# A second weight kept whole in DRAM and split on chip, and two start points moved later

## Chip, cores and metric

One Trainium2 chip, one of its cores. The metric is the device time of one execution in microseconds (us), lower is better. The kernel before takes 1595.91 us (median of 3 runs, 1595.83 to 1598.31).

## Reference

```python
def _attn_ref(q, k, v, p):            # 8 batches x 8 heads x 576 rows x 64; p has 32 rows a head
    p_packed = sm_attn(p, k, v)       # 32 rows attend to the 576 keys
    return sm_attn(q, p_packed, p_packed)

def _moe_ref(x, w_in, w_out):         # 4608 x 512, d_ff 2048
    h = x @ w_in
    return (h - np.tanh(h)) @ w_out

def _moe2_ref(x, w_in, w_out, s, b):
    r = np.maximum(x @ w_in, 0.0)
    return (s * (r * r) + b) @ w_out
```

The attention's output, with its heads laid side by side, goes through the first MLP and the result through the second. The weights arrive as 64-bit floats, which the kernel holds as pairs of 32-bit integers and converts by itself.

## The kernel before

**Numbers.** A float32 operand of a matrix product is split into a high part (rounded to the reduced format of TensorE) and the low rest, and each product is three matmuls: high by low, high by high, low by high. "Split" below means one ScalarE copy (the high part) and one VectorE subtraction (the low part).

**First half: attention and first MLP.** Eight batches run in turn, each in two halves of 288 tokens. `attention()` makes each batch's packed keys (`stage1`), its combined weights (`make_z`) and its second attention (`second_stage`). `mm1` and `mm2` are the first MLP's two products, 16 column blocks `j` for each half batch. TensorE's main stream is the loop over `j`; everything else is a Python generator of which the loop advances one step at a time through `slot()`. What order instructions get on an engine is therefore fixed when the program is built, and every engine works its list in that order.

**Weights of the first MLP.** In the first batch w_in1 and w_out1 are converted from 64 bits by `to_f32` (one ScalarE `Abs`, then four VectorE operations) while the first attention runs. `w1_steps` does w_in1, `wo1_steps` w_out1, which it also splits (`split_wo`). The first two pairs of w_out1 blocks stand in the generator `rest`, and the loop over `both([first_z(0), second_stage(0, 0)])` advances `rest` by one step for each of its own.

**Weights of the second MLP.** The second MLP uses Strassen's scheme with seven products (P1 to P7), for which seven combinations of the four blocks of each weight are needed. `second_weights()` (the generator `more`, one step in every third slot) loads 32 pieces of both weights into `w2s`, converts them into `cv`, forms the combinations, splits them and stores both parts to DRAM, in `w2_d` (w_in2, pieces 0 to 15) and `wo2_d` (w_out2, pieces 16 to 31).

**Second half: `SecondMLP`.** `run()` goes through 6 blocks of tokens by 4 steps `k`, seven products of 12 matmuls each, with w_in2's 28 units held in SBUF. Its results (`g`) go to DRAM and come back (`B<-g`) for `second()`, the product with w_out2: 6 blocks of 28 steps of 12 matmuls. During the last block of `run()` the 28 SBUF places come free one by one, and `load_unit4` fills them with units of w_out2 by DMAs that the POOL engine issues. `late(n, step)` is the part of a `run()` step that is put off into the next one: its VectorE sums, its stores of `g` and the product P4. The g buffers are reused from step to step, so a new sum waits until the store of the old one has landed.

In `second()` the inputs are split six steps ahead (`LOOK`), by `split_hi` on ScalarE and `split_lo` on VectorE.

Of the kernel before, what the change touches and what calls it, by code (L numbers as in the profile page):

```python
# [8 lines left out]
F32 = mybir.dt.float32  # L9
F32R = mybir.dt.float32r  # L10
# [3 lines left out]
ALU = mybir.AluOpType  # L14
# [4 lines left out]
def pack_attention_two_mlps(ctx, tc, q, k, v, p, w_in1, w_out1, w_in2, w_out2, s_in, b_in, out):  # L19
# [10 lines left out]
    nc = tc.nc  # L30
# [4 lines left out]
    P = 128  # L35
# [13 lines left out]
    FT = FF // (2 * P)  # L49
# [3 lines left out]
    LAND = 14  # L53
    W_K, W_P, W_PK, W_PV, W_E, W_Q = 2, 9, 5, 1, 7, 3

    AFTER, SLOTS = (3, 4, 1, 1), (0, 1, 4, 1)
    AHEAD, CATCH_UP = 13, 11
    EXP_LO, EXP_HI = 2.0 ** -15, 2.0 ** 16 * 1.875
    assert 2 * R == P and NB == 2 * C and 4 * M == P and 2 * D == P and H * D == DM

# [1 line left out]
    dram = ctx.enter_context(tc.tile_pool(name="dram", bufs=1, space=bass.MemoryType.DRAM))  # L62
# [14 lines left out]
    bias = const.tile([P, KD], F32, name="bias")  # L77
    csum = apool.tile([P, 2, P], F32, name="csum")

    w2_d = [dram.tile([7, P, 2, 2, 2, P], F32, name=f"w2_d{k}") for k in range(FT // 2)]  # L80
    wo2_d = [dram.tile([7, P, 2, 2, 2, P], F32, name=f"wo2_d{k}") for k in range(FT // 2)]
    g2_d = [[dram.tile([P, FT // 2, 2, TH], F32, name=f"g2_{i}_{n}") for n in range(7)] for i in range(NBK2)]
    x2t = dram.tile([P, KD, NT], F32, name="x2t")

# [370 lines left out]
    def both(gens):  # L455
        gens = list(gens)
        while gens:
            for g in list(gens):
                try:
                    next(g)  # L460
                except StopIteration:
                    gens.remove(g)
                    continue
                yield
# [14 lines left out]
    with tc.manual_schedule():  # L479
# [66 lines left out]
        def first_z(c):  # L546
            while ("z", c) not in granted:
                yield
            yield from make_z(0, c)
            done.add(("z", 0, c))  # L550

        def second_stage(b, hf):
            yield from scores2(b, hf)
            yield from both([stage2(b, hf, g) for g in range(G)])
            done.add(("a", b, hf))
# [49 lines left out]
        load_q(0, 1)  # L605
        until(("w1", 0, 1), conv)
        rest = seq(conv, in_turn([(wo1_steps, 0), (wo1_steps, 1)], [(wo1_steps, 2), (wo1_steps, 3)]))
        for _ in both([first_z(0), second_stage(0, 0)]):
            next(rest, None)
        nc.sync.dma_start(out=s_sb, in_=s_in.partition_broadcast(P))  # L610
        nc.sync.dma_start(out=b_sb, in_=b_in.partition_broadcast(P))

# [15 lines left out]
        def second_weights():  # L628

            both_ = wslot(I64, "w2s", [P, 8, P])
            N = 4 * FT

            def unit(n):
                if n >= 2 * FT:
                    i, f = (n - 2 * FT) // FT, n % FT
                    return w_out2, FT * P, f * P, i * P, FF // 8, f, i, wo2_d[f // 2][:, :, f % 2]
                f, i = n // 2, n % 2
                return w_in2, 2 * P, i * P, f * P, FF // 2, f, i, w2_d[f // 2][:, :, f % 2]  # L640

            def load(n):
                if n < N:
                    src, half, r0, c0, cols = unit(n)[:5]
                    for kh in range(2):
                        rr = src[kh * half + r0:kh * half + r0 + P].rearrange("p (h c) -> p h c", h=2)
                        t = both_[:, n % 2 * 4 + 2 * kh:n % 2 * 4 + 2 * kh + 2]
                        nc.sync.dma_start(out=t, in_=rr[:, :, c0:c0 + P])

            load(0)  # L650
            yield
            for n in range(N):
                out2 = n >= 2 * FT
                f, i, dst = unit(n)[5:]
                load(n + 1)
                yield
                t = both_[:, n % 2 * 4:n % 2 * 4 + 4]
                hi = t.bitcast(F32).rearrange("p a c -> p (a c)")[:, :7 * P]
                xa = cv[:, 7:11] if n % 2 else cv[:, 0:4]
                yield from to_f32(xa, t, xa.bitcast(I32))  # L660
                if out2:
                    if f == 0:
                        nc.gpsimd.memset(csum, 0.0)
                    for kh in range(2):
                        nc.gpsimd.tensor_tensor(out=csum, in0=csum, in1=xa[:, 2 * kh:2 * kh + 2], op=ALU.add)

                nc.vector.tensor_tensor(out=cv[:, 4], in0=xa[:, 1], in1=xa[:, 3], op=ALU.add)
                yield
                nc.vector.tensor_tensor(out=cv[:, 5], in0=cv[:, 4], in1=xa[:, 0], op=ALU.subtract)
                yield  # L670
                nc.vector.tensor_tensor(out=cv[:, 6], in0=xa[:, 2], in1=cv[:, 5], op=ALU.subtract)
                yield
                nc.vector.tensor_tensor(out=xa[:, 1], in0=xa[:, 0], in1=xa[:, 1], op=ALU.subtract)
                yield
                x = (cv[:, 4:11] if n % 2 else cv[:, 0:7]).rearrange("p a c -> p (a c)")
                nc.scalar.copy(hi.bitcast(F32R), x)
                yield
                nc.vector.tensor_tensor(out=x.bitcast(F32R), in0=x, in1=hi, op=ALU.subtract)
                yield
                for hl, v in enumerate((hi, x)):  # L680
                    v = v.rearrange("p (c x) -> p c x", c=7)
                    for c0, c1, at in ((0, 4, 3), (4, 7, 0)) if n % 2 else ((0, 7, 0),):
                        nc.sync.dma_start(out=dst[c0:c1, :, hl, i].rearrange("c p x -> p c x"),
                                          in_=v[:, at:at + c1 - c0])
                if out2 and f == FT - 1:
                    ps = bank_h(f"cs_{i}")
                    for h in range(2):
                        nc.tensor.matmul(ps[:, 2 * h:2 * h + 2], csum[:, h], ones, start=True, stop=True)
                    for h in range(2):
                        m = 2 * h + i  # L690
                        nc.vector.tensor_scalar(out=bias[:, m:m + 1], in0=ps[:, 2 * h:2 * h + 1], scalar1=b_sb,
                                                scalar2=None, op0=ALU.mult)
                    yield
# [59 lines left out]
        for b in range(B):  # L753
# [4 lines left out]
            for hf, js in parts:  # L758
# [10 lines left out]
                for j in js:  # L769
                    c = j // CH  # L770
# [11 lines left out]
                    t = act1(h, f"{b}_{hf}_{j}")  # L782
# [27 lines left out]
class SecondMLP:  # L810
# [21 lines left out]
    def __init__(self, tc, ctx, wslot, w2_d, wo2_d, x2t, g2_d, s_sb, bias, out):  # L832
        self.tc, self.nc, self.ctx, self.wslot = tc, tc.nc, ctx, wslot
        self.w2_d, self.wo2_d, self.x2t, self.g2_d = w2_d, wo2_d, x2t, g2_d
        self.s_sb, self.bias, self.out = s_sb, bias, out
        self.P, self.TH = 128, g2_d[0][0].shape[3]
        self.NBK, self.NK = len(g2_d), len(w2_d)

        self.units = []
        for k in range(self.NK):  # L840
            for p in self.ORDER[:2] + (("P4",) if k else ()) + self.ORDER[2:6]:
                self.units.append((k - 1 if p == "P4" else k, p))
        self.units.append((self.NK - 1, "P4"))
        self.place, self.w2, self.w4 = [], {}, {}
        self.next4 = 0
        pool = ctx.enter_context(tc.tile_pool(name="early", bufs=1, side="right"))
        self.raw = {n: pool.tile([128, 2, self.TH], F32, tag=n, name=n) for n in ("B11", "B12", "B22", "B21")}
        self.xs = [pool.tile([128, 2, 2, self.TH], F32R, tag=f"x{n}", name=f"x{n}") for n in range(4)]
        px = ctx.enter_context(tc.tile_pool(name="px", bufs=1, space=bass.MemoryType.PSUM, side="right"))
        self.X = px.tile([128, 2, 512], F32, tag="x", name="X")  # L850
# [21 lines left out]
    def load_unit4(self):  # L872

        n = self.next4
        p, k = self.ORDER4[n // self.NK], n % self.NK
        self.w4[p, k] = self.place[n]
        self.nc.gpsimd.dma_start(out=self.place[n].bitcast(F32), in_=self.wo2_d[k][self.W[p]])
        self.next4 += 1

    def slots_for(self, t):  # L880
        n = len(self.place)
# [91 lines left out]
    def run(self):  # L973
# [15 lines left out]
        for n in range(NP):  # L989
# [12 lines left out]

            def freed():
                if last:
                    self.load_unit4()

            if n:
# [94 lines left out]
    def second(self, NP):  # L1102
# [52 lines left out]
                                         start=first and p in ("P1", "P5", "P6"), stop=last, skip_group_check=True)  # L1155

        for n, (i, p, k) in enumerate(self.steps[:-self.NK]):
            while self.split < min(len(self.steps), n + self.LOOK):
                self.split_step()
            if k == 1 and outs:  # L1160
                emit(*outs.pop())
            if k == 0 and n:
                after(*self.steps[n - 1][:2])
            multiply(n, range(2))
            if n < 3:
                self.late(NP - 1, n)
            if n == 4:
                self.late(NP - 1, 3)
                self.stream += self.g[3:]
            if n >= 2 and n % 3 and self.next4 < len(self.units):  # L1170
                self.load_unit4()

        after(*self.steps[-self.NK - 1][:2])
# [40 lines left out]
```

## Time and profile before

| | |
|---|---|
| median of the runs | 1595.91 us |
| the profiled execution | 1598.22 us, of which its trace spans 1596.5 us |
| TensorE busy | 1483.3 us, 93% of the span |
| VectorE busy | 1088.6 us, 68% |
| ScalarE busy | 743.0 us, 47% |
| mean granted TensorE clock | 0.976 of full speed |

Three stretches matter. From 0 to about 210 us the first batch starts up; in the 40 us slices of the page TensorE is busy 40 to 70% there. From 210 to 1160 us it is busy nearly without a gap. From 1160 to 1250 us `run()` hands over to `second()`, and one slice there falls to 70%. After that TensorE is full again until the last stores.

### The profile page before, as it was taken

What the parts mean: (1) busy time and instruction counts of PE and PEld (TensorE: products, weight loads), DVE (VectorE), ACT (ScalarE), POOL (GpSimd) and SP (SyncE); (2) the same over time, 40 slices, a digit from 0 to 9 for tenths busy, and PEclk for the clock granted to TensorE, in tenths of its full rate; (3) what the DMA queues carried; (4) which work ended last, traced back from release to release, by engine and by line L of the source; (5) the groups of instructions that cost most, each with busy time, mean ns of one, the idle gap of its engine ahead of it and who ended that gap; (6) DMA issues with size and microseconds to landing.
All of it is one profiled execution on the core that took longest, in us unless ns stands there. A gap on an engine that the chain in (4) does not pass through costs nothing.

```text
span 1596.5 us, 27039 instructions
## 1 busy us (share of the span) xinstructions
PE 1483.3 (93%) x9976; PEld 1389.4 (87%) x9976; DVE 1088.6 (68%) x2076; ACT 743.0 (47%) x1417; POOL 108.4 (7%) x143
## 2 busy tenths in 40 slices
PE   4477799999999999999999999999997999999998
PEld 2366588898888888988899999999997999999998
DVE  4888486877879687786844677677754665565564
ACT  2444244444444444444433556566554554454452
POOL 0234100000000000000202000000021000000000
PEclk9689899999999999999999999999999899999999
DMA  8844645374554645453624664655589886786683
GB/s 163 192 133 110 128 118 145 95 165 120 117 146 120 148 111 124 142 127 109 185 98 187 237 246 181 234 218 203 220 340 394 281 235 187 219 251 187 211 252 80
DMA packets 396372, 285.70 MB, mean 179 GB/s; under 512 B 243664, under 2 KB 341968, under 8 KB 396240
## 3 DMA queue, kind: packets, MB, share of 16 engines
q1 hardware_dynamic: 387648, 254.03, 54.2%
q0 software_dynamic: 8064, 29.36, 5.0%
q8 instruction: 78, 1.28, 0.3%
q10 hardware_dynamic: 528, 0.59, 0.1%
q14 instruction: 54, 0.44, 0.1%
HBM read 168.43 MB, written 115.47 MB: 178 GB/s over the span
## 4 chain that ended last, share of the span: by engine, by line
PE 72%; DVE 10%; DMA 8%; SPq 4%; issue 3%; ACT 2%; DVEq 0%; ACTq 0%
PE acc L427 19%; PE Y L1154 9%; PE h L404 9%; PE Y L939 8%; PE Z L1154 6%; PE X L1154 6%; PE X L939 5%; PE Z L939 5%; DMA g<-g 3%; PE zp L318 2%; SPq L197 1%; DMA q<-in_q_dram 1%; DVE gl L133 1%; DMA w1s<-in_moe_w_in_dram 1%; PE pv L292 1%
## 5 line engine op out<-in xcount | busy, mean ns | idle before, releaser
L427 PE MATMUL acc<-gh,wo 128*128 128x288 f32 x2040 | 422.3, 298 | 0.0
L427 PEld LDWEIGHTS acc<-gh,wo 128*128 128x128 f32 x2040 | 333.5, 191 | 0.0
L427 PE MATMUL acc<-gl,wo 128*128 128x288 f32 x1020 | 314.7, 309 | 6.9 <-POOL gl L133 6.5
L412 ACT ACTIVATE t<-h 128x288 f32<-128x288 f32 x256 | 105.1, 410 | 306.8 <-PE h L404 264.3
L427 PEld LDWEIGHTS acc<-gl,wo 128*128 128x128 f32 x1020 | 194.5, 191 | 46.6 <-issue 31.2
L413 DVE TENSOR_TENSOR t<-h,t 128x288 f32<-128x288 f32 x256 | 115.8, 452 | 165.9 <-ACT t L412 164.9
L404 PE MATMUL h<-a2h,z 128*128 128x288 f32 x1024 | 216.4, 299 | 6.7 <-DVE z L385 6.7
L854 DVE TENSOR_TENSOR x<-B,x 128x768 fp32r<-128x768 f32 x158 | 147.1, 950 | 88.0 <-ACT x L1088 75.0
L404 PE MATMUL h<-a2l,z 128*128 128x288 f32 x512 | 155.1, 303 | 20.2 <-DVE a2l L369 18.6
L404 PEld LDWEIGHTS h<-a2h,z 128*128 128x128 f32 x1024 | 167.3, 192 | 7.3 <-DVE z L385 7.3
L939 PE MATMUL Y<-x,w 128*128 128x384 f32 x864 | 160.7, 339 | 9.0 <-DVE g L854 8.2
L939 PEld LDWEIGHTS Y<-x,w 128*128 128x128 f32 x864 | 152.7, 190 | 10.0 <-DVE g L854 8.5
L1154 PE MATMUL Y<-x,w 128*128 128x384 f32 x864 | 153.2, 335 | 0.7 <-DVE s L854 0.7
L1154 PEld LDWEIGHTS Y<-x,w 128*128 128x128 f32 x864 | 150.3, 188 | 1.0 <-DVE s L854 1.0
L404 PEld LDWEIGHTS h<-a2l,z 128*128 128x128 f32 x512 | 98.6, 193 | 26.0 <-DVE a2l L369 20.1
L1088 ACT CAST x<-B 128x768 fp32r<-128x768 f32 x116 | 93.7, 833 | 50.3 <-DMA B<-g 27.6
L939 PE MATMUL Z<-x,w 128*128 128x384 f32 x576 | 109.6, 339 | 4.4 <-DVE u L854 4.4
L132 ACT CAST gh<-t 128x288 fp32r<-128x288 f32 x255 | 108.5, 426 | 1.2 <-DVE t L413 1.2
L939 PE MATMUL X<-x,w 128*128 128x384 f32 x576 | 108.0, 336 | 0.0
L939 PEld LDWEIGHTS Z<-x,w 128*128 128x128 f32 x576 | 102.3, 191 | 4.7 <-DVE u L854 4.7
L1154 PE MATMUL X<-x,w 128*128 128x384 f32 x576 | 102.8, 337 | 0.0
L1154 PE MATMUL Z<-x,w 128*128 128x384 f32 x576 | 102.0, 335 | 0.0
(148 smaller groups left out, 2047.8 us busy)
## 6 DMA issues: line engine op xcount, KB each, us to landing
g<-g SPq DMA_DIRECT2D x196, 384.0 KB, 3.5
B<-g SPq DMA_DIRECT2D x116, 384.0 KB, 4.6
w<-w_d POOLq DMA_DIRECT2D x28, 512.0 KB, 7.2
w<-wo_d POOLq DMA_DIRECT2D x28, 512.0 KB, 8.4
k<-in_k_dram SPq DMA_DIRECT2D x128, 72.0 KB, 3.0
q<-in_q_dram SPq DMA_DIRECT2D x256, 36.0 KB, 2.1
B<-x2t SPq DMA_DIRECT2D x24, 384.0 KB, 5.4
g<-s SPq DMA_DIRECT2D x24, 384.0 KB, 2.7
```

Of the source, the lines that this page charges most:

```text
L132: nc.scalar.copy(hi, x)
L133: (eng or nc.vector).tensor_tensor(out=lo, in0=x, in1=hi.bitcast(F32), op=ALU.subtract)
L197: nc.sync.dma_start(out=t[p0:p0 + 32], in_=src.rearrange("(n r) d -> r n d", r=32))
L318: nc.tensor.matmul(ps[e][i * M:(i + 1) * M, :rhs(i).shape[-1]], pblk[b][r, h // 4, h % 4 * M:h % 4 * M + M], rhs(i)[r], start=True, stop=True)
L404: nc.tensor.matmul(h[:, :HB], zt[:, zi, g, f0:f0 + P], a[:, g], start=(n == 0), stop=(n == 3 * G - 1))
L412: nc.scalar.activation(t, h[:, :HB], AF.Tanh)
L413: nc.vector.tensor_tensor(out=t, in0=h[:, :HB], in1=t, op=ALU.subtract)
L427: nc.tensor.matmul(acc[m][:, :HB], w[:, m * P:(m + 1) * P], x, start=(j == js[0] and i == 0), stop=(j == js[-1] and i == 2))
L854: self.nc.vector.tensor_tensor(out=o, in0=a, in1=b, op=op)
L939: self.nc.tensor.matmul(bank[:, f, :self.TH], w[:, f, a, kt], x[:, b, kt], start=(p in ("P1", "P5", "P6") and m == 0), stop=(m == 5), skip ...
L1088: self.nc.scalar.copy(self.xs[(7 * self.NBK + n) % self.XS][:, 0], self.ready[0])
L1154: nc.tensor.matmul(bank[:, ft, :T], w[:, kk, u, ft], x[:, v, kk], start=first and p in ("P1", "P5", "P6"), stop=last, skip_group_check=True)
```

## The change

Three edits. First, w_out2's combinations are no longer split before they are stored: `wo2_d` holds one float32 number in place of two parts, a unit's load is 256 KB in place of 512 KB, and lands in the half of the unit's place that will be the low part. A new function `split_unit4` makes the high part of one unit on ScalarE and subtracts it on VectorE one call later. It is called before each of the later twelve `load_unit4` of `run()`, and then in `second()`. The loads in `second()` are issued in each step rather than in two of three.

Second, the loop over `first_z(0)` and `second_stage(0, 0)` begins to advance `rest` only after its first 16 steps (`FIRST`). Third, `second_weights()` waits `LAND` = 14 of its steps after its first load, in place of one.

```diff
-    AHEAD, CATCH_UP = 13, 11
+    AHEAD, CATCH_UP, FIRST = 13, 11, 16
...
-    wo2_d = [dram.tile([7, P, 2, 2, 2, P], F32, name=f"wo2_d{k}") for k in range(FT // 2)]
+    wo2_d = [dram.tile([7, P, 2, 2, P], F32, name=f"wo2_d{k}") for k in range(FT // 2)]
...
-        for _ in both([first_z(0), second_stage(0, 0)]):
-            next(rest, None)
+        for i, _ in enumerate(both([first_z(0), second_stage(0, 0)])):
+            if i >= FIRST:
+                next(rest, None)
...
             load(0)
-            yield
+            yield from wait(LAND)
...
-                nc.scalar.copy(hi.bitcast(F32R), x)
-                yield
-                nc.vector.tensor_tensor(out=x.bitcast(F32R), in0=x, in1=hi, op=ALU.subtract)
-                yield
-                for hl, v in enumerate((hi, x)):
+                if not out2:
+                    nc.scalar.copy(hi.bitcast(F32R), x)
+                    yield
+                    nc.vector.tensor_tensor(out=x.bitcast(F32R), in0=x, in1=hi, op=ALU.subtract)
+                    yield
+                for hl, v in enumerate((x,) if out2 else (hi, x)):
...
-        self.nc.gpsimd.dma_start(out=self.place[n].bitcast(F32), in_=self.wo2_d[k][self.W[p]])
+        self.nc.gpsimd.dma_start(out=self.place[n][:, :, 1].bitcast(F32), in_=self.wo2_d[k][self.W[p]])
         self.next4 += 1
+
+    def split_unit4(self):
+
+        n = self.split4
+        if n:
+            t = self.place[n - 1]
+            self.sub(t[:, :, 1], t[:, :, 1].bitcast(F32), t[:, :, 0].bitcast(F32))
+        if n < len(self.units):
+            t = self.place[n]
+            self.nc.scalar.copy(t[:, :, 0], t[:, :, 1].bitcast(F32))
+        self.split4 += 1
...
             def freed():
                 if last:
+                    if self.next4 > 2:
+                        self.split_unit4()
                     self.load_unit4()
...
         for n, (i, p, k) in enumerate(self.steps[:-self.NK]):
+            while self.split4 <= min(len(self.units), n + 4):
+                self.split_unit4()
...
-            if n >= 2 and n % 3 and self.next4 < len(self.units):
+            if n >= 2 and self.next4 < len(self.units):
                 self.load_unit4()
```

On ScalarE, at the first batch's start (`z` is the first combined weight, `wo1s` a 64-bit block of w_out1, `t_0_0_0` the softmax of the second attention), the list before reads:

```order
L96 COPY pblk_348<-pkT_0_344 128x128
L117 ACTIVATE t_395<-wo1s_201 128x512
L117 ACTIVATE t_399<-wo1s_203 128x512
L383 CAST z_0_384<-zp_0_0_385 128x512
L383 CAST z_0_384<-zp_0_1_386 128x512
L117 ACTIVATE t_417<-wo1s_205 128x512
L117 ACTIVATE t_419<-wo1s_207 128x512
L136 CAST wo_0_423<-wo1s_201 128x512
L136 CAST wo_1_425<-wo1s_203 128x512
L347 ACTIVATE t_0_0_0_439<-t_0_0_0_439 128x288
```

In the changed kernel the same place of ScalarE's list reads:

```order
L97 COPY pblk_348<-pkT_0_344 128x128
L384 CAST z_0_384<-zp_0_0_385 128x512
L384 CAST z_0_384<-zp_0_1_386 128x512
L118 ACTIVATE t_424<-wo1s_201 128x512
L118 ACTIVATE t_427<-wo1s_203 128x512
L348 ACTIVATE t_0_0_0_417<-t_0_0_0_417 128x288
L348 ACTIVATE t_0_0_1_420<-t_0_0_1_420 128x288
L118 ACTIVATE t_442<-wo1s_205 128x512
```

The casts of `z` have moved ahead of the first two reads of w_out1, and the softmax ahead of the second two.

Still on ScalarE, where the first batch ends and the second one's attention begins (`cv<-w2s` is the first step of `second_weights()`, `e_1_0` the packed attention of batch 1), the list before reads:

```order
L412 ACTIVATE t_0_15_1398<-h_0_15_1379 128x288
L132 CAST gh_0_0_15_1401<-t_0_14_1314 128x288
L117 ACTIVATE cv<-w2s 128x512
L265 ACTIVATE e_1_0_1393,nm_0_1427<-s_1_0_0_1428,nm_0_1427 128x5x32
L265 ACTIVATE e_1_0_1393,nm_0_1427<-s_1_0_0_1428,nm_0_1427 128x4x32
```

In the changed kernel the attention follows directly, and the read of `w2s` stands here, after the attention of both head groups:

```order
L368 CAST a2h_0_1782<-a_1_0_1_1776 128x288
L384 CAST z_2_1811<-zp_2_0_1812 128x512
L384 CAST z_2_1811<-zp_2_1_1813 128x512
L413 ACTIVATE t_1_14_1826<-h_1_14_1778 128x288
L133 CAST gh_0_1_14_1829<-t_1_13_1749 128x288
L118 ACTIVATE cv<-w2s 128x512
```

It has moved behind everything that the second batch's attention needs of ScalarE for its first half.

The third place is the last block of `run()` on ScalarE in the changed kernel (`g` and `u` are its squares, `s` the copy of a product, `w_0`, `w_1` pairs of units):

```order
L868 ACTIVATE g_10518<-g_10518 128x768
L891 CAST w_0_9967<-w_0_9967 128x2x256 x2
L867 ACTIVATE g_10515<-X 128x768
L868 ACTIVATE g_10515<-g_10515 128x768
L891 CAST w_1_9970<-w_1_9970 128x2x256
L867 ACTIVATE u_10514<-u_10514 128x768
L868 ACTIVATE u_10514<-u_10514 128x768
L891 CAST w_1_9970<-w_1_9970 128x2x256
```

Before, the squares followed each other there without a cast of `w` between them.

## Rows read from the trace of the kernel before

**Rows 1.** Windows: busy us of each engine, clock, DMA share, GB/s.

```profile
1200.00:1240.00 40.00, 27.85 (x149) 26.90 (x147) 19.44 (x23) 16.82 (x21) 5.28 (x10) 0.90 0.97 376
1280.00:1320.00 40.00, 40.00 (x232) 40.00 (x231) 24.49 (x30) 21.22 (x28) 0.00 (x0) 1.00 0.83 251
```

**Rows 2.** Timeline of PE, 1150 to 1250 us: start, length, instructions, [idle before].

```profile
1179.65 4.36 PE L939 MATMUL Y<-x,w 128*128 128x384 f32 x24
...
1194.29 4.36 PE L939 MATMUL Y<-x,w 128*128 128x384 f32 x24
...
1215.49 4.34 PE L939 MATMUL Y<-x,w 128*128 128x384 f32 x24
...
1240.52 4.21 PE L939 MATMUL Y<-x,w 128*128 128x384 f32 x12 [8.18 <-DVE g L854]
```

**Rows 3.** The chain that ended last, 1150 to 1260 us: start, length.

```profile
1199.44 10.28 DMA g<-g
...
1229.48 9.24 DMA B<-g
```

**Rows 4.** DMA, 1163 to 1245 us: queues as in part 3; issues, us to landing.

```profile
q1 hardware_dynamic: 5589, 15.30, 47.2%
q0 software_dynamic: 3888, 14.16, 46.7%
...
w<-wo_d POOLq DMA_DIRECT2D x27, 512.0 KB, 8.4
g<-g SPq DMA_DIRECT2D x27, 384.0 KB, 7.3
```

**Rows 5.** DMA issues, 900 to 1160 us.

```profile
g<-g SPq DMA_DIRECT2D x108, 384.0 KB, 2.6
```

**Rows 6.** The page's DMA issues, whole span.

```profile
B<-g SPq DMA_DIRECT2D x116, 384.0 KB, 4.6
...
k<-in_k_dram SPq DMA_DIRECT2D x128, 72.0 KB, 3.0
```

**Rows 7.** Timeline of POOL, last block of run().

```profile
1188.47 0.53 POOL L877 DMA_DIRECT2D w<-wo_d  x1 [1.55 <-PE Z L939]
```

**Rows 8.** DMA queues, 640 to 680 us: packets, MB, share of 16 engines.

```profile
q1 hardware_dynamic: 9675, 5.64, 49.0%
```

**Rows 9.** The page's costliest groups: VectorE's splits of inputs.

```profile
L854 DVE TENSOR_TENSOR x<-B,x 128x768 fp32r<-128x768 f32 x158 | 147.1, 950 | 88.0 <-ACT x L1088 75.0
```

**Rows 10.** Timeline of ACT, 18 to 66 us.

```profile
37.27 0.66 ACT L117 ACTIVATE t<-wo1s 128x512 f32<-128x512 f32 x1 [5.29 <-DMA wo1s<-in_moe_w_out_dram]
...
41.34 1.06 ACT L383 CAST z<-zp 128x512 fp32r<-128x512 f32 x2
...
59.33 2.19 ACT L117 ACTIVATE w<-w1s 128x1024 f32<-128x1024 f32 x2
```

**Rows 11.** Timeline of PE, 18 to 62 us.

```profile
32.13 1.52 PE L318 MATMUL zp<-w,pblk 64*32 64x512 f32 x16
...
59.61 0.61 PE L404 MATMUL h<-a2l,z 128*128 128x288 f32 x1 [11.45 <-DVE a2l L369]
```

**Rows 12.** Timeline of SP's queue, 18 to 80 us.

```profile
36.08 9.34 SPq L146 DMA_DIRECT2D w1s<-in_moe_w_in_dram  x8
```

**Rows 13.** Tile w1s, 30 to 64 us.

```profile
DMA to landing us min/median/max: 8.7/11.6/13.4
```

**Rows 14.** Timeline of ACT, 135 to 215 us.

```profile
166.98 0.66 ACT L117 ACTIVATE cv<-w2s 128x512 f32<-128x512 f32 x1 [7.92 <-DMA w2s<-in_moe_w_in_dram]
```

**Rows 15.** Timeline of PE, 155 to 180 us.

```profile
169.14 1.11 PE L272 MATMUL e1Tp<-ident,e 128*128 128x128 f32 x4 [7.38 <-ACT e L265]
```

**Rows 16.** Timeline of DVE, 135 to 215 us.

```profile
160.91 0.22 DVE L260 TENSOR_SCALAR nm<-nm 128x1 f32<-128x1 f32 x1
...
177.31 0.47 DVE L246 STREAM_TRANSPOSE kT<-k 128x288 f32<-128x288 f32 x1
```

**Rows 17.** Timeline of SP's queue, 0 to 210 us.

```profile
164.65 5.70 SPq L170 DMA_DIRECT2D k<-in_k_dram  x8
```

More of the change, by code (lines that the diff above doesn't have):

```diff
@@ L675, in second_weights @@
                 x = (cv[:, 4:11] if n % 2 else cv[:, 0:7]).rearrange("p a c -> p (a c)")
-                nc.scalar.copy(hi.bitcast(F32R), x)
-                yield
-                nc.vector.tensor_tensor(out=x.bitcast(F32R), in0=x, in1=hi, op=ALU.subtract)
-                yield
-                for hl, v in enumerate((hi, x)):
+                if not out2:
[4 more added lines that the diff above has]
+                for hl, v in enumerate((x,) if out2 else (hi, x)):
                     v = v.rearrange("p (c x) -> p c x", c=7)
                     for c0, c1, at in ((0, 4, 3), (4, 7, 0)) if n % 2 else ((0, 7, 0),):
-                        nc.sync.dma_start(out=dst[c0:c1, :, hl, i].rearrange("c p x -> p c x"),
-                                          in_=v[:, at:at + c1 - c0])
+                        to = dst[c0:c1, :, i] if out2 else dst[c0:c1, :, hl, i]
+                        nc.sync.dma_start(out=to.rearrange("c p x -> p c x"), in_=v[:, at:at + c1 - c0])
                 if out2 and f == FT - 1:
@@ L844, in __init__ @@
         self.place, self.w2, self.w4 = [], {}, {}
-        self.next4 = 0
+        self.next4 = self.split4 = 0
         pool = ctx.enter_context(tc.tile_pool(name="early", bufs=1, side="right"))
```

## Prediction

> **What bounds the kernel now.** I read the page's slices first, since they show where TensorE is not full, then the windows of those stretches, the chain that ended last inside them, and the timelines of the engine that waits and the one it waits for. TensorE runs the sum of its matmuls almost without a gap from 210 to 1160 us and from 1250 us to the end, so whatever the change adds or takes on other engines there is worth nothing unless it makes TensorE wait. Three places are left, and each edit touches one.
>
> Place one is the hand-over from `run()` to `second()`. In its 40 us TensorE is busy for 27.85 us and the DMA engines for 97% of the time at 376 GB/s [rows 1]. The chain there is not compute: it is the landing of stores of `g` (10.28 us for one) and of a load `B<-g` (9.24 us) [rows 3]. The same store takes 2.6 us while `run()` is in its steady state [rows 5] and 7.3 us here [rows 4]. What has come on top is POOL's queue: 27 loads of w_out2, 46.7% of sixteen engines' time over 82 us [rows 4]. TensorE's own rows give the loss. A pair of Y products comes every 14.64 us (1179.65 to 1194.29); the next was due at 1208.93 and came at 1215.49, 6.56 us late. Then it stands idle for 8.18 us, and the 12 matmuls after that take 4.21 us where 24 took 4.36 us, 2.0 us more than their share [rows 2]. Together 16.7 us.
>
> Place two is the start. ScalarE waits 5.29 us for a block of w_out1 and reaches the casts of `z` at 41.34 us [rows 10], although TensorE had their input done at 32.13 + 1.52 = 33.65 us; TensorE's first `h` then starts at 59.61 us after 11.45 us of idleness [rows 11]. Place three is the second batch's attention: ScalarE waits 7.92 us for the first load of w_in2 [rows 14], while the softmax behind it had its input at 161.13 us [rows 16], and TensorE stands for 7.38 us until that softmax is through [rows 15].
>
> **Term one, half as many bytes in place one.** A unit's load cost 46.7% of 16 engines over 82 us, 612.7 engine-us for 3888 packets: 157.6 ns for a packet of 3642 bytes, and 612.7/27/16 = 1.42 us of all sixteen engines a load [rows 4]. After the change a unit lands in two runs of 1 KB in each of 128 partitions, 256 pieces. No load of POOL in this trace has such pieces, so I bound their price. From below: the mixed small packets of 640 to 680 us, 5.64 MB in 9675 or 583 bytes on average, took 0.49 x 16 x 40 us / 9675 = 32.4 ns [rows 8]. From above: a whole old packet, 157.6 ns. A straight line between the two gives 50 ns at 1 KB, and since a kilobyte lies nearer to 583 bytes than to 3642 I take that. A load is then 256 x 50/16 = 0.80 us, 0.62 us less, 16.7 us less over 27 loads: of the 82 us the DMA engines had about 77 us of work (47.2% and 46.7% [rows 4]), and would have 60. With a quarter of the time free, a store should land nearer to 2.6 us than to 7.3 us, and the 6.56 us go. The 8.18 us go only in part: `second()` begins with loads `B<-g` on which ScalarE, and behind it VectorE and TensorE, must wait in order. With the page's median of 4.6 us [rows 6] in place of 9.24 us, 8.18 - 4.64 = 3.5 us of idleness stay. Term one is 16.7 - 3.5 = 13 us; its ends are 16.7 us and, if pieces cost as much as old packets, a loss (below).
>
> Here a rule can be weighed against the rows. The Trainium skill, "DMA: Bandwidth & Descriptors", sections "Anatomy of one DMA — SWDGE (gpsimd) path" and "Bandwidth", fits a POOL-issued transfer as 2.0 us fixed plus its bytes at 436 GB/s, and tells authors to batch towards 1 MiB; by that estimate 512 KB costs 3.2 us and 256 KB 2.6 us, so that halving a load saves a fifth; 27 loads would then give back 7.7 us of 82, term one would be 6 us, and the kernel would take 1580 us. The row has 1.42 us of all engines for 512 KB, less than the fit's fixed part alone, so a good part of that lies outside the engines' busy time here; none of this trace's rows shows 256 KB on POOL's queue.
>
> **What the split adds.** 28 ScalarE copies and 28 VectorE subtractions of 512 elements. VectorE takes 950 ns for 768 elements [rows 9], so 0.63 us here, 17.7 us in all, and ScalarE's copies I put no higher. Sixteen steps of `second_weights()` lose a copy and a subtraction of 896 elements each in return, under a full TensorE, worth nothing. The cover of the added work: 17 splits fall into 17 steps of `second()`, 17 x 2.09 = 35 us of TensorE (14.64/7 us for a product), where VectorE was busy 24.49 of 40 us [rows 1]; 21.7 + 10.7 = 32 of 35 us still fits, and inputs are split six steps ahead. Eleven or twelve fall into the last block of `run()`, whose idle VectorE time was itself waiting for stores. A copy waits for its load on an engine that works in order, and behind it stand the squares that `late` and P4 need. But it is called three `freed()` later than its load, and 15 such calls in four passes of 14.64 us are 3.9 us apart: 11.7 us against 8.4 us to landing when the queues were full [rows 4]. I cost this at nothing, up to 2 us. Where `load_unit4` stands in `second()` doesn't matter: POOL has nothing else to do, and issues when TensorE gives up a place [rows 7].
>
> **Term two, FIRST.** ScalarE meets the casts of `z` before it waits for w_out1. At most the chain to the first `h` moves up by 41.34 - 33.65 = 7.7 us. VectorE still has all four conversions to do, and TensorE needs w_out1 soon after, but that work fills waits. The next limit is a transfer that compute doesn't move: the second quarter of w_in1, issued from 36.08 to 45.4 us [rows 12] and landing 11.6 us later [rows 13], is there at 57.0 us; its conversion began its second half at 59.33 + 2.19/2 = 60.4 us [rows 10]. So 3.4 us at least for the second combined weight if everything else keeps pace. I take 4 us, ends 0 (VectorE, which was nearly full, gives it back) and 7.7.
>
> **Term three, LAND.** ScalarE's wait leaves the path: the read of `w2s` goes behind the second batch's attention, and lands long before it is due. The gain is at most TensorE's 7.38 us. What is late next is the second head group's `k`: its eight DMAs were issued from 164.65 us for 5.70 us [rows 17], 0.71 us each; without the second piece's two DMAs ahead of them they end at 168.9 us, land 3.0 us later [rows 6], and two transposes (0.94 us) end at 172.9 us where they ended at 177.78 us [rows 16]: 4.9 us. Between 4.9 and 7.4 I take 6. The conversion moved behind that point meets a full TensorE and costs nothing.
>
> **Sum.** 13 + 4 + 6 = 23 us. The profiled execution took 1598.22 us, 1596.5 us of it span; its span becomes 1573.5 us and its own time 1575. The median of the runs is 2.3 us below that execution, so I forecast 1595.9 - 23 = 1573 us.
>
> **Rivals.** *The queues stay full.* A piece of 89 ns would make a load cost what it did (1.42 x 16/256). At 70 ns, halfway from my 50, a load takes 1.12 us, 27 loads give back 8 us rather than 16.7, the DMA engines still have 69 of 82 us of work, and stores still land late. Term one shrinks to 13 x 8/16.7 = 6 us: 1580 us. For it speaks that no such load is in the trace; against it that small packets cost little at 640 us [rows 8]. The page of the Trainium skill named above would come out at the same time.
>
> *The start gives its gains back.* VectorE's list in the first 160 us has the same work in another order. If terms two and three come to nothing, 1583 us; with term three at 4.9 us alone, 1578 us. Against it: all three waits are on transfers, not on a full engine.
>
> *Pieces cost as much as packets (slower).* 256 x 157.6/16 = 2.52 us a load, 1.10 us more, 30 us over 27 loads in a stretch without room: minus the 10 us of the start, 20 us slower, 1616 us. It decides from 0.37 us more a load, 112 ns a piece, which is over three times the small packets of rows 8.
>
> *It doesn't matter.* Everything is hidden elsewhere, 1594 to 1598 us. TensorE's waits in all three places name what the edits remove, so this is unlikely.
>
> **Chances and range.** My forecast with its own spread of 1565 to 1577 us: 0.60. Queues full (1577 to 1583): 0.15. Start given back (1577 to 1585): 0.12. More than forecast (below 1565): 0.05. No change: 0.04. Slower: 0.04. The range 1564 to 1584 us leaves out about 0.15. A measurement of this kernel can tell 0.2%, 3.2 us, from no change; by the cases faster 0.92, same 0.04, slower 0.04.
>
> **What would show it.** Right: 28 loads of 256 KB on POOL's queue with a share well under 30% of the same stretch, stores `g<-g` back to 3 to 4 us, no idleness over 4 us on TensorE between 1160 and 1240 us; first `h` on TensorE at 52 to 56 us; no wait of ScalarE for `w2s`, and e1Tp less than 2 us after the matmuls before it. Wrong: ScalarE waiting in `split_unit4` for `wo_d`, VectorE's subtractions of `w` ahead of a TensorE wait, a share of POOL's queue as before, or TensorE idle at 70 to 100 us for w_out1 that is now converted too late.

## The result, and the profile after

The changed kernel takes 1571.16 us (median of 4 runs, 1569.75 to 1572.55) beside 1595.87 us for the kernel before (4 runs, 1593.48 to 1598.31): a ratio of 0.9845, 95% interval 0.9826 to 0.9864, or 24.7 us less. The profiled execution took 1572.55 us, 1570.8 us of it span.

First the hand-over. Windows of the changed kernel, with the columns of [rows 1]:

```profile
1160.00:1200.00 40.00, 40.00 (x232) 40.00 (x231) 28.08 (x34) 25.14 (x34) 13.75 (x20) 1.00 0.96 351
1200.00:1240.00 40.00, 35.87 (x197) 35.55 (x197) 27.48 (x34) 25.73 (x37) 2.97 (x5) 0.96 0.88 312
1240.00:1280.00 40.00, 40.00 (x232) 40.00 (x232) 33.32 (x47) 25.38 (x39) 0.00 (x0) 1.00 0.76 218
```

TensorE is full up to 1200 us, and the worst 40 us hold 35.87 us of work in place of 27.85 [rows 1]. VectorE, which now splits w_out2 too, is busiest behind that, 33.32 of 40 us, while TensorE has no gap there. TensorE's timeline of the same stretch:

```profile
1165.47 4.36 PE L953 MATMUL Y<-x,w 128*128 128x384 f32 x24
...
1194.75 4.36 PE L953 MATMUL Y<-x,w 128*128 128x384 f32 x24
...
1203.11 2.27 PE L953 MATMUL Y<-x,w 128*128 128x384 f32 x12
1205.22 6.40 PE L1170 MATMUL X<-x,w 128*128 128x384 f32 x36
1215.75 3.92 PE L953 MATMUL Y<-x,w 128*128 128x384 f32 x12 [4.13 <-DVE g L857]
```

The pairs of Y keep their 14.64 us (two of them from 1165.47 to 1194.75), so the 6.56 us of lateness [rows 2] are gone. The stall before the last P4 is 4.13 us in place of 8.18, and those 12 matmuls still run slow, 3.92 us where half of 4.36 would be 2.18. The window of those 12 matmuls (PEclk, the granted clock, is the third number from the end) has it at 0.56, most of the stretch at the lower of the two levels (1.2 and 2.4 GHz), right behind 4.13 us without work:

```profile
1215.75:1219.60 3.85, 3.85 (x13) 3.85 (x14) 2.21 (x3) 3.12 (x4) 0.00 (x0) 0.56 0.35 140
```

The chain that ended last shows what the stall is:

```profile
1204.95 8.03 DMA B<-g
...
1214.75 0.96 DVE g L857
1215.75 3.92 PE Y L953 x12
```

No store of g stands there any more [rows 3]; one load B<-g does, at 8.03 us. The DMA view, 1138 to 1230 us, with the columns of [rows 4]:

```profile
q1 hardware_dynamic: 7664, 20.94, 59.5%
q0 software_dynamic: 2240, 7.34, 25.7%
...
g<-g SPq DMA_DIRECT2D x34, 384.0 KB, 4.7
w<-wo_d POOLq DMA_DIRECT2D x28, 256.0 KB, 5.8
B<-g SPq DMA_DIRECT2D x14, 384.0 KB, 6.3
```

These are 92 us, and [rows 4] are 82 us. The line of POOL's queue in the kernel before over 92 us, 1154 to 1246 us, is:

```profile
q0 software_dynamic: 3888, 14.16, 41.6%
```

So over equal lengths POOL's queue takes 25.7% in place of 41.6%. A store of g takes 4.7 us in place of 7.0 (7.3 in [rows 4]).

At the start, ScalarE's timeline has the cast of z ahead of the waits for w_out1 [rows 10], and TensorE's first h comes 7.5 us earlier than in [rows 11]:

```profile
34.91 1.07 ACT L384 CAST z<-zp 128x512 fp32r<-128x512 f32 x2 [2.63 <-PE zp L319]
37.40 0.70 ACT L118 ACTIVATE t<-wo1s 128x512 f32<-128x512 f32 x1 [1.41 <-DMA wo1s<-in_moe_w_out_dram]
```

```profile
52.10 0.61 PE L405 MATMUL h<-a2l,z 128*128 128x288 f32 x1 [13.88 <-DVE a2l L370]
```

In the second batch ScalarE reads w2s 30 us later and without a wait, and TensorE's idleness of 7.38 us [rows 15] is 1.06 us. Timelines of ScalarE, TensorE and VectorE, in that order:

```profile
196.50 0.70 ACT L118 ACTIVATE cv<-w2s 128x512 f32<-128x512 f32 x1
```

```profile
157.65 0.66 PE L273 MATMUL e1Tp<-ident,e 128*128 128x128 f32 x4 [1.06 <-ACT e L266]
...
167.09 1.57 PE L229 MATMUL s<-kT,ppT 128*64 128x288 f32 x6 [2.01 <-DVE kT L247]
```

```profile
163.79 0.84 DVE L247 STREAM_TRANSPOSE kT<-k 128x288 f32<-128x288 f32 x2 [1.60 <-DMA k<-in_k_dram]
...
166.56 0.48 DVE L247 STREAM_TRANSPOSE kT<-k 128x288 f32<-128x288 f32 x1 [1.93 <-DMA k<-in_k_dram]
```

What is late next is the second head group's k, as the forecast said.

### The profile page after: what moved, and what is told of

It reads as the page before. It is cut to its first block, busy times and chain, and to the rows that moved or that the text cites. A ratio compares the mean times of both kernels' runs of the same rounds, so it can differ in the third digit from the quotient of the medians.

```text
span 1570.8 us, 26999 instructions
## 1 busy us (share of the span) xinstructions
PE 1483.8 (94%) x9976; PEld 1391.6 (89%) x9976; DVE 1091.3 (69%) x2088; ACT 742.1 (47%) x1429; POOL 115.2 (7%) x143
## 4 chain that ended last, share of the span: by engine, by line
PE 76%; DVE 11%; SPq 4%; DMA 4%; issue 3%; ACT 2%; POOL 0%; ACTq 0%; DVEq 0%
PE acc L428 18%; PE Y L1170 10%; PE Y L953 9%; PE h L405 9%; PE Z L1170 6%; PE X L953 6%; PE Z L953 6%; PE X L1170 6%; PE zp L319 2%; SPq L198 2%; DVE gl L134 1%; PE pv L293 1%; SPq L171 1%; PE s L229 1%; DVE t L414 1%
## 5 line engine op out<-in xcount | busy, mean ns | idle before, releaser
L134 DVE TENSOR_TENSOR gl<-t,gh 128x288 fp32r<-128x288 f32 x224 | 103.8, 464 | 0.0
```

The costliest lines, as they stand in the source:

```text
L134: (eng or nc.vector).tensor_tensor(out=lo, in0=x, in1=hi.bitcast(F32), op=ALU.subtract)
```

## The experiments

The theory is the forecast's: three separate waits, each worth its own term. The rivals are that the terms overlap, that the hand-over gained by something other than bytes, and that the added split costs something. Each kernel ran beside the kernel before on the same chip (four or five runs each; the kernel before has seven to nine):

| kernel | median us | before us | ratio, 95% interval |
|---|---|---|---|
| float32 w_out2 alone | 1583.43 | 1596.57 | 0.9920, 0.9907 to 0.9934 |
| start edits alone | 1586.42 | 1596.57 | 0.9938, 0.9926 to 0.9951 |
| changed, FIRST undone | 1576.16 | 1596.57 | 0.9878, 0.9864 to 0.9892 |
| changed, LAND undone | 1580.40 | 1596.57 | 0.9905, 0.9891 to 0.9919 |
| units loaded twice | 1582.26 | 1596.34 | 0.9918, 0.9904 to 0.9931 |
| inputs loaded earlier | 1574.27 | 1596.34 | 0.9860, 0.9846 to 0.9873 |
| that, and k ahead of q | 1568.18 | 1596.34 | 0.9821, 0.9807 to 0.9834 |
| split done twice | 1581.11 | 1596.34 | 0.9904, 0.9890 to 0.9917 |
| sum ahead of the splits | 1567.44 | 1595.42 | 0.9826, 0.9811 to 0.9841 |
| that, and k ahead of q | 1563.46 | 1595.42 | 0.9801, 0.9785 to 0.9817 |
| no split | 1573.25 | 1595.42 | 0.9866, 0.9849 to 0.9883 |
| loads in two of three steps | 1571.59 | 1596.63 | 0.9848, 0.9830 to 0.9867 |

### The parts by themselves

Only the edits to w_out2, with both start points as before:

```diff
-    AHEAD, CATCH_UP, FIRST = 13, 11, 16
+    AHEAD, CATCH_UP, FIRST = 13, 11, 0
...
-            yield from wait(LAND)
+            yield
```

> Only the float32 copy of w_out2 and its split; both start points as before. If the 11 us that the changed kernel's trace shows between 1165 us and the end belong to the lighter loads: 1585 us, stores of g in the hand-over at 4 to 5 us, the first 500 us as before. If the 3.7 us gained between 210 and 835 us come from the pieces of w_out2 that lost two steps (they begin at about 500 us): 1581 us. Rival, the gain in the hand-over came from the earlier start (other phase of the transfers): 1594 to 1598 us.

Measured: 13.1 us less, 1583.43 us, between the 1585 and the 1581 us of the first two cases. The opposite kernel keeps the old w_out2 and has the two start points alone:

> Only FIRST = 16 and LAND = 14; w_out2 stored split as before. If the start's gains reach the end: 1585.4 us (10.5 us less), with the idle times in the hand-over as before (some 8 us before a half-speed Y, stores of g at 7 us). If the 3.7 us of the steady state come from the new order at the start too: 1582 us. Rival, the start gives its gains back: 1590 to 1596 us.

Measured: 10.2 us less, as in the first case. 13.1 and 10.2 make 23.3 us, the whole change gives 24.7 us, and the intervals (some 2 us each) cover the difference: the start's gain reaches the end, and the parts add. The hand-over behaves accordingly. TensorE's timeline of the kernel with w_out2 alone, then of the one with the start alone:

```profile
1224.95 3.58 PE L953 MATMUL Y<-x,w 128*128 128x384 f32 x12 [4.22 <-DVE g L857]
```

```profile
1227.97 3.79 PE L940 MATMUL Y<-x,w 128*128 128x384 f32 x12 [8.02 <-DVE g L855]
```

Without the lighter loads the 8 us stall is there, whatever the start did.

A smaller part of the 13.1 us lies elsewhere. One window, 600 to 835 us, of the kernel before, of the start alone, of w_out2 alone and of the changed kernel; the pieces of w_out2 are made in this stretch:

```profile
600.00:835.00 235.00, 230.09 (x1804) 209.25 (x1803) 170.13 (x441) 101.82 (x268) 22.27 (x33) 1.00 0.47 128
```

```profile
600.00:835.00 235.00, 230.08 (x1806) 209.83 (x1805) 175.12 (x440) 103.71 (x269) 22.83 (x35) 1.00 0.48 135
```

```profile
600.00:835.00 235.00, 231.64 (x1816) 212.40 (x1815) 158.35 (x419) 93.51 (x258) 20.51 (x31) 0.99 0.40 107
```

```profile
600.00:835.00 235.00, 232.09 (x1839) 213.54 (x1838) 163.63 (x424) 95.54 (x263) 23.16 (x35) 1.00 0.41 113
```

With unsplit pieces alone VectorE has some 12 us and ScalarE 8 us less to do, and TensorE is busy for 1.6 to 2.0 us more in the same 235 us. That is small, but it is in both kernels with the lighter pieces and in neither of the others. A window at fixed times holds slightly different work in each kernel, so a cut by events is safer.

Such a cut is the store of `x2t`, the tile in DRAM in which the first half leaves its output. SP's queue issues 17 of them in each kernel, and the first and the last split each profiled execution into three parts, of which the third holds `run()` and `second()`. The last of them, before and then changed:

```profile
832.59 0.57 SPq L445 DMA_DIRECT2D x2t<-xs  x1
```

```profile
818.41 0.53 SPq L446 DMA_DIRECT2D x2t<-xs  x1
```

| kernel | us to the first store | first to last | last to the end of the span |
|---|---|---|---|
| before | 108.08 | 724.51 | 763.9 |
| start edits alone | 103.03 | 718.16 | 762.0 |
| float32 w_out2 alone | 105.31 | 722.21 | 752.5 |
| changed, FIRST undone | 105.56 | 715.87 | 752.6 |
| changed, LAND undone | 102.35 | 722.48 | 752.2 |
| changed | 102.54 | 715.87 | 752.4 |

The last column separates the kernels with the lighter loads from the others: 9.6 to 11.4 us. The middle one gives the lighter pieces 2.3 us in both pairs (724.51 - 722.21 and 718.16 - 715.87).

Then the changed kernel with one start point undone at a time, by the two lines of the diff above.

> The changed kernel with FIRST = 0. If the cast of z behind the wait for w_out1 is worth what the changed trace shows (about 5.3 us at 140 us): 1576.5 us, first h at 59 to 60 us again. Rival, the two start edits overlap, and the later one would have made up for the first: 1571 to 1573 us.

> The changed kernel with the wait of LAND steps undone. If the wait of ScalarE for w_in2's first load was on the path for its whole size less what comes behind it (about 5.2 us): 1576.4 us, ScalarE waiting some 8 us for w2s ahead of the softmax. Rival, the steady state has room to make it up: 1571 to 1573 us.

Measured: FIRST undone costs 5.0 us (1576.16 beside 1571.16), first h at 58.37 us; LAND undone costs 9.2 us, more than the 5.2 us expected. These two differences set runs beside each other that were not made together. Set against w_out2 alone, on the same chip, FIRST is worth 1583.43 - 1580.40 = 3.0 us and LAND 1583.43 - 1576.16 = 7.3 us. The spans of the profiled executions (w_out2 alone 1580.0, LAND undone 1577.0, FIRST undone 1574.0, changed 1570.8) give 3.0 and 3.2 us for FIRST, 6.0 and 6.2 us for LAND. The table agrees with the smaller figures: up to the first store FIRST gives 3.0 us in both pairs (105.31 - 102.35 and 105.56 - 102.54) and nothing more behind it, and LAND gives 6.3 to 6.6 us between the first and the last store. So FIRST is worth about 3 us and LAND 6 to 7 us (3 to 5 and 6 to 9 by the medians), and neither makes up for the other.

FIRST moves the first h by 58.37 - 52.10 = 6.3 us, twice what it is worth. The products `zp` of the second combined weight, for which TensorE waits until VectorE has converted w_in1's second quarter, move by 2.4 us only. TensorE's timeline with FIRST undone, then changed:

```profile
67.69 1.09 PE L319 MATMUL zp<-w,pblk 64*32 64x512 f32 x16 [1.39 <-DVE w L128]
```

```profile
65.26 1.09 PE L319 MATMUL zp<-w,pblk 64*32 64x512 f32 x16 [0.69 <-DVE w L128]
```

With LAND undone ScalarE's wait and TensorE's behind it are back (timelines of ScalarE and TensorE):

```profile
160.89 0.66 ACT L118 ACTIVATE cv<-w2s 128x512 f32<-128x512 f32 x1 [7.19 <-DMA w2s<-in_moe_w_in_dram]
```

```profile
163.05 1.11 PE L273 MATMUL e1Tp<-ident,e 128*128 128x128 f32 x4 [6.65 <-ACT e L266]
```

### Bytes, or something else?

Each unit is loaded a second time into the half that the high part then overwrites:

```diff
+        self.nc.gpsimd.dma_start(out=self.place[n][:, :, 0].bitcast(F32), in_=self.wo2_d[k][self.W[p]])
         self.nc.gpsimd.dma_start(out=self.place[n][:, :, 1].bitcast(F32), in_=self.wo2_d[k][self.W[p]])
```

> The changed kernel, but each unit of w_out2 is loaded twice, once into the half that the high part then overwrites: 512 KB a unit again, in 256 KB loads, and nothing else changed. If the bytes of these loads in the hand-over are what the float32 copy saves: POOL's queue at or over its old 47% in the hand-over, stores of g at 7 us or more, and the 11 to 13 us come back: 1582 to 1586 us. Rival, the gain comes from the order of the loads or the pieces of the store: 1570 to 1573 us.

Measured: 1582.26 us, 11.1 us more than the changed kernel. The DMA view of 1138 to 1230 us, and TensorE's timeline:

```profile
q0 software_dynamic: 4320, 14.16, 41.4%
...
w<-wo_d POOLq DMA_DIRECT2D x56, 256.0 KB, 7.9
g<-g SPq DMA_DIRECT2D x30, 384.0 KB, 6.7
```

```profile
1195.81 3.81 PE L954 MATMUL Z<-x,w 128*128 128x384 f32 x12 [5.09 <-DVE u L857]
...
1224.57 4.21 PE L954 MATMUL Y<-x,w 128*128 128x384 f32 x12 [8.15 <-DVE g L857]
```

14.16 MB are on POOL's queue again, as in [rows 4], and both old stalls are back, although the pieces, the split and the order of the loads are the changed kernel's. Its share of 41.4% is that of the kernel before over an equal 92 us, 41.6%; the 47% expected was taken from 82 us. From the last store of `x2t` to the end the kernel takes 764.1 us, as the kernel before does (763.9). ScalarE never waits for a unit of w_out2 there, so the second load doesn't act by holding up the split. The traffic of these loads is what the hand-over gained by. The number of loads isn't it, since 28 loads before and 56 here give the same stalls; bytes and packets go up together (3888 packets before, 2240 changed, 4320 here), and the runs don't tell these two apart.

### Does the added split cost anything?

First each ScalarE copy and each VectorE operation of the split is doubled, without changing the numbers; then both are left out (the bodies of `split_unit4` do nothing, and the second product is taken with parts of w_out2 that are not the right ones).

```diff
             self.sub(t[:, :, 1], t[:, :, 1].bitcast(F32), t[:, :, 0].bitcast(F32))
+            self.add(t[:, :, 1], t[:, :, 1].bitcast(F32), t[:, :, 1].bitcast(F32), ALU.max)
...
             self.nc.scalar.copy(t[:, :, 0], t[:, :, 1].bitcast(F32))
+            self.nc.scalar.copy(t[:, :, 0], t[:, :, 1].bitcast(F32))
```

> The changed kernel with the added split done twice: 28 more copies on ScalarE and 28 more operations of the same size on VectorE (0.6 us each), same result. If the split is hidden under TensorE, as the forecast costed it: 1569 to 1573 us. Rival, VectorE has no room there: up to 18 us more, 1575 to 1589 us.

> The changed kernel without the added split: the high and low parts of w_out2 are left as whatever lies there, so the second product is left wrong in its values while its matmuls stay. If the split is hidden, as the forecast costed it: 1569 to 1573 us. Rival, part of it lies on the path in the hand-over, where doubling it cost 9.5 us: 1562 to 1568 us.

Measured: doubled 1581.11 us, 10 us more; left out 1573.25 us, no gain, and just above the 1569 to 1573 us of the first case. From the last store of `x2t` to the end the kernel without a split takes 752.3 us, as the changed one does (752.4), and the doubled one 763.6 us. One split of each unit is hidden, two aren't. The window and TensorE's timeline of the doubled kernel show where the cover ends:

```profile
1240.00:1280.00 40.00, 35.80 (x183) 33.86 (x182) 35.59 (x50) 28.43 (x46) 0.00 (x0) 0.91 0.62 178
```

```profile
1271.94 8.98 PE L1172 MATMUL Y<-x,w 128*128 128x384 f32 x34 [2.79 <-DVE w L857]
```

VectorE at 35.59 of 40 us makes TensorE wait for the subtraction of w itself. The expectation's first theory, that double would be hidden too, failed: the cover was there once and was nearly used up by that.

The loads of `second()` in two of three steps again (`n % 3` put back into the condition):

> The changed kernel with the loads in second() issued in two of three steps again. If POOL's loads start only when TensorE gives up a place, and TensorE needs a unit many steps later, as the forecast argued: 1569 to 1573 us. Rival, the later loads hold up ScalarE's copies of the split, and behind them the inputs: 1575 us or more, with ScalarE waiting for wo_d.

Measured: 1571.59 us, the same. Whether these loads are issued in each step or in two of three makes no difference here.

### What remains of the stall

If B<-g comes late, it should help to load it earlier: `free_loads` is set for the whole last step of `run()`.

```diff
+            self.free_loads = last and end
...
-        self.free_loads = True
```

> The changed kernel, but the inputs of second() from the fifth on are loaded during the last step of run() as buffers come free, not only from the start of second(). If the 4.1 us of idleness and the half-speed Y behind it (1.8 us) come from the late load B<-g: 4 to 6 us less, 1565 to 1567 us. Rival, the earlier loads only delay the stores of g, on which the same sum waits: 1571 us or more.

Measured: 1574.27 us, no gain, and TensorE's stall as before:

```profile
1216.82 4.21 PE L953 MATMUL Y<-x,w 128*128 128x384 f32 x12 [4.67 <-DVE g L857]
```

The edit hardly moved the loads. The first of them was issued at 1203.00 us beside 1204.08 us, but the buffers for B come free only as VectorE splits what is in them: between 1195 and 1225 us SP's queue waited for those splits for 4.9 us in all, beside 5.0 us in the changed kernel. The load for which the sum waited landed at 1215.2 us, not earlier than the changed kernel's 1213.0 us. So this run doesn't show what loads that land earlier would give. VectorE's own list in the changed kernel shows what TensorE waits for:

```profile
1212.06 0.96 DVE L857 TENSOR_TENSOR x<-B,x 128x768 fp32r<-128x768 f32 x1 [3.10 <-ACT x L1104]
1213.87 0.96 DVE L857 TENSOR_TENSOR x<-B,x 128x768 fp32r<-128x768 f32 x1 [0.86 <-ACT x L1104]
1214.75 0.95 DVE L857 TENSOR_TENSOR g<-Y,q 128x768 f32<-128x768 f32 x1
```

P4 adds to the Y bank that the sum g<-Y,q must read first. That Y was done at 1203.11 + 2.27 = 1205.4 us, but the sum stands behind two splits of inputs five and six steps ahead, and those wait for B<-g. So the lookahead is shortened for three steps, and the loads are issued without it:

```diff
-            while self.split < min(len(self.steps), n + self.LOOK):
+            if n == 0:
+                while self.stream:
+                    self.load_step()
+            while self.split < min(len(self.steps), n + (self.LOOK if n > 2 else 4)):
```

> The changed kernel; in second() the inputs are split only four steps ahead for the first three steps, then six, with the loads B<-g issued at once. VectorE then reaches the sum g<-Y,q, for which the last P4 waits, ahead of the two splits that wait for B<-g. If that order, not the loads, is what leaves 4.1 us of idleness and a half-speed Y: 4 to 6 us less than the changed kernel, 1565 to 1568 us. Rival, the inputs come too late for the fourth and fifth step then: the idleness moves there, 1570 to 1574 us.

Measured: 1567.44 us, 28.0 us under the kernel before on its chip where the changed kernel, measured at another time, had 24.7: some 3 us less, a little short of 4 to 6, and the two intervals overlap. The profiled executions settle it: from the last store of `x2t` to the end this kernel takes 748.1 us, 4.3 us less than the changed one. VectorE's and TensorE's timelines:

```profile
1207.83 0.96 DVE L857 TENSOR_TENSOR x<-B,x 128x768 fp32r<-128x768 f32 x1 [1.49 <-ACT x L1104]
1208.71 0.95 DVE L857 TENSOR_TENSOR g<-Y,q 128x768 f32<-128x768 f32 x1
```

```profile
1211.29 2.24 PE L953 MATMUL Y<-x,w 128*128 128x384 f32 x12
...
1234.06 1.15 PE L1170 MATMUL X<-x,w 128*128 128x384 f32 x5 [1.43 <-DVE w L857]
```

The stall and the slow P4 are gone (2.24 us for 12 matmuls, with the granted clock at 1.00 from 1211.3 to 1213.5 us); 1.43 us come back at 1234 us, where TensorE waits for the split of w, which now has less slack.

### What is late after LAND

On the kernel with earlier inputs, and again on the one with the sum first, the second batch's loads of q and the first load of w_in2 go behind those of k:

```diff
             load_k(*then_k)
+            if (b, g) == (1, 0):
+                load_q(1, 0)
...
-            load(0)
-            yield from wait(LAND)
+            yield from wait(LAND - 4)
+            load(0)
+            yield from wait(4)
```

> As the one before, and in the second batch the loads of q and the first load of w_in2 are issued behind those of the second head group's k. If k is what is late next after LAND (1.60 and 1.93 us of VectorE's waits, 2.01 us of TensorE's): 1.3 to 3.6 us less than the one before, 1562 to 1565 us, with no wait of VectorE for k near 165 us. Rival, q is then late by as much: no difference from the one before.

> As the one before, and with the loads of q and of w_in2 behind those of k in the second batch. If the two gains add: 1559 to 1563 us. Rival, they overlap: 1564 to 1568 us.

Measured: 1568.18 us, 6.1 us less than without it where 1.3 to 3.6 were expected, and 1563.46 us, 4.0 us less, at the edge of the 1559 to 1563 us at which the gains add. VectorE has no wait for k near 165 us any more. SP's queue and TensorE's timeline of the first of them:

```profile
152.96 5.31 SPq L171 DMA_DIRECT2D k<-in_k_dram  x8
```

```profile
168.45 1.11 PE L275 MATMUL e1Tp<-ident,e 128*128 128x128 f32 x4 [2.42 <-ACT e L268]
```

k is issued 4.9 us earlier than the changed kernel's 157.88 us, and the group's e1Tp, at 172.50 us there, starts 4.05 us earlier. That is the size of the gain on the second kernel; what the first got beyond it is about the width of the intervals, and its cause is open. With both edits the kernel takes 1563.46 us, 32.0 us under the kernel before, and is the fastest version run.

## Why the prediction was right, and where its steps were off

**The sum.** 23 us were forecast, 24.7 us came. Between the terms no errors cancel: w_out2 was put at 13 us and gave 13.1 us alone, the start at 10 us and gave 10.2 us alone. Inside the first term some do, and that it came out within 0.1 us is partly luck: the hand-over gave less than forecast, and a place put at nothing made up for it.

**Term one, the bytes.** The price of a load was nearly right, by luck, since both factors of it were wrong. From 25.7% of 16 engines over 92 us a load took 0.257 x 16 x 92/28/16 = 0.84 us of all engines, where the forecast had 0.80 and the kernel before 1.42. But a load made 2240/28 = 80 packets of 3.3 KB on average, not 256 pieces of 1 KB, and each took 169 ns rather than 50. The transfers were cheaper because there were fewer packets, at nearly the old price each. The rival in which a piece costs as much as a packet fell with the count. The engines did not get the quarter of free time that was forecast: over 82 us of the changed kernel, 1149 to 1231 us, POOL's queue used 28.9% and the other one 60.1%, since more stores and loads of g fall into the same time once TensorE no longer waits. The 6.56 us of lateness went all the same.

The Trainium skill's rule weighed in the prediction ("DMA: Bandwidth & Descriptors", section "Anatomy of one DMA — SWDGE (gpsimd) path", a fixed 2.0 us and bytes at 436 GB/s for one transfer) led to an estimate of 6 us for term one. For loads that are in flight together the trace disagrees with that estimate, since the engines' time fell by 41% for half as many bytes and the term came to 13.1 us.

**Term one, what stays.** In the hand-over itself the gain was 16.7 - 4.1 - 1.7 = 10.9 us: the 6.56 us went, the idleness left was 4.13 us where the forecast had 3.5, and the slow P4 after it, which the forecast struck out, stayed (3.92 us, 1.7 us too long, at a granted clock of 0.56 behind the idleness that the forecast itself had left). The step that failed is the one on B<-g. It was to land in 4.6 us, the median of the whole execution; it took 8.03 us on the chain and 6.3 us by the median of the stretch. The words "must wait in order" were right, but the forecast drew from them only that the loads should land sooner: moving the sum ahead of two splits removed the stall, although the loads were issued at about the same time (1203.90 us beside 1204.08 us). The missing 2 us of the term came from a place the forecast put at nothing, the pieces of w_out2 under a TensorE that was only nearly full: 2.3 us by the stores of `x2t`.

**The split.** Costed at nothing, and leaving it out gains nothing. The working (32 of 35 us of VectorE's time) also says how little room was left, and doubling it cost 10 us.

**Terms two and three.** FIRST: 4 us forecast, about 3 measured. The first h moved by 6.3 us, but the conversion of w_in1's second quarter, which the forecast named as the next limit, began on ScalarE only 58.09 - 54.52 = 3.6 us earlier than with FIRST undone (3.4 us were forecast), and VectorE's part of it left 2.4 us for the second combined weight. LAND: 6 us forecast, 6 to 7 measured, with the wait for k behind it as named; putting k first gave 4 to 6 us more.

**The signs.** Stores of g came to 4.7 us, not to 3 to 4, and the idleness of 4.13 us was just over the 4 us allowed. It isn't the queue of the stores alone that makes them slower: in the steady state of the kernel before, 900 to 1160 us, the same queue used 55.3% of the engines and a store took 2.6 us [rows 5], and here it used 59.5%, with the 25.7% of POOL's queue on top. POOL's share was under 30%, but over 82 us (28.9%) only just. The other signs came as named.

## What to carry to other kernels

Where a hand-over is limited by transfers, count the bytes of every queue in that stretch: halving one queue's bytes took some 10 us off here, and giving the bytes back took the gain back. An engine that works in order turns one late load into a stall for work that doesn't need it, so before loading earlier, look what stands behind the waiting instruction; three rows of VectorE's list told more than the landing time did. Work that is hidden once needn't be hidden twice: check the busy time of the covering stretch, not the average.

## What the runs showed that was not expected

A 256 KB load whose rows land in two runs of 1 KB went out as 80 packets of 3.3 KB on average. Its issue on POOL took longer than that of 512 KB, 716 ns by the median beside 0.53 us [rows 7]. POOL's timeline has the median in the middle of three (tile wo_d):

```profile
L880 POOL DMA_DIRECT2D w<-wo_d x28: 704/716/728, 1149.2 to 1220.0; - x28
```

Equal instructions can differ by some us from one profiled execution to another; whether the execution or the chip makes the difference isn't known, since the traces were not all taken on one chip. The kernel before and the one with w_out2 alone have the same work up to about 500 us, and yet the first store of x2t comes 2.8 us apart (SP's queue, before and then w_out2 alone):

```profile
108.08 0.57 SPq L445 DMA_DIRECT2D x2t<-xs  x1
```

```profile
36.02 7.97 SPq L147 DMA_DIRECT2D w1s<-in_moe_w_in_dram  x8
...
105.31 0.57 SPq L446 DMA_DIRECT2D x2t<-xs  x1
```

Eight loads of w_in1 were issued in 7.97 us there and in 9.34 us in [rows 12]. So what a start edit gains can't be read from two traces alone: the trace of before against that of after gives 108.08 - 102.54 = 5.5 us at that store, where the single parts give 3.0, and so the runs of single parts were needed.
